# A scan and two expert layers on one core: one warm-up product, first weights loaded first and rounded early, fourth weight tile ahead of the sums' write, probabilities later

## The chip, the core and the metric

The kernel runs on one core of a Trainium2 chip. Its engines are TensorE (PE; its weight loads are shown as PEld), VectorE (DVE), ScalarE (ACT), GpSimd (POOL) and SyncE (SP), which here only issues transfers. The metric is the device time of one execution in microseconds. Each engine works through its own list of instructions in order; an instruction waits until what it needs has been signalled, and what stands behind it waits with it.

## What is computed

Three layers follow one another: a chunked scan with decay, a mixture of four experts with ReLU, and a dense layer with a gate. Cut to what matters:

```
log_a = log(clip(a, 1e-6, 1))                 # a: 4 x 8 heads x 768 positions
cum   = cumsum(log_a) within a chunk
M     = (C @ B^T) * exp(cum_i - cum_j), causal
y     = M @ x + (C @ state) * exp(cum)        # state carried over chunks
state = exp(sum log_a) * state + sum(B x^T * exp(cum_end - cum_j))
x     = y as 3072 tokens x 256
p     = domain_probs / sum(domain_probs)      # 3072 x 4
x     = sum_e p_e * (relu(x @ w1[e]) @ w2[e]) # F = 1024
out   = (silu(x @ wg) * (x @ wv)) @ wo        # F = 1536
```

The kernel uses chunks of 128 positions, which gives the same result.

## The kernel before

**Tiles.** The scan is done in 24 tiles of 128 tokens (`q` = 0 to 23). Each holds for 8 heads a table `L` of 128 x 128 decays, which is turned by ScalarE into exponentials and multiplied by scores (products of B and C). The products of these weights with x give the tokens of the expert layer. Experts 0 and 1 start as soon as the first two tiles of the scan are there; the other scan tiles are worked in between their products. A unit is one expert, one token block and one of eight columns of hidden features: six products of L616 into one of three banks `h`, from which ScalarE makes `hh` (ReLU, rounded, L657) and VectorE the rest `hl` (L658); three units later six products of L624 add up the output. A bank `h` is taken again three units later, when `hh` and `hl` are both made.

**Two parts of each number.** fp32 numbers are multiplied as a high part (rounded by ScalarE) and a low part (what is left, by VectorE or GpSimd). So each weight tile of 512 KB has to be loaded, rounded (`high`, L268, or L158) and subtracted (`low`, L272, or L162) before L616 or L624 can use it. A weight tile (e, part) is loaded by `expert_load` (L180); parts 0 and 2 are the first layer of expert e, parts 1 and 3 the second.

**The first two scan tiles** go a direct way in `begin` (from L284): warm-up products on `ones` (L1161), four masks (`first_mask`, L198), running sums of log a by a product with a triangle (`sums`, `cum`), rows of these sums added to the masks (`first_rows`, L205), scores (`first_scores`, L221), exponentials (`first_direct`, `first_exp`), weights (`first_weights`, L257), and then the products with x (`a_heads`, L539). The other tiles get their table `L` from DRAM: the sums are copied by ScalarE (`crow`, L328), written to `crow_d` (L329), and read back spread over all partitions (`a_load_cum`, L412). GpSimd cuts what lies above the diagonal (`a_causal`, L419), ScalarE takes exponentials (`a_exp`, L426). The scores of the third and fourth tile go into a bank `direct` (`direct_scores`, L221), which is the bank of the first two tiles' output and state sums `y01`; VectorE copies the state sums out as `st` (`a_keep`, L557).

**What sets the order.** The order on each engine is that of the code (`manual_schedule`); work between the units is put into numbered half-unit slots by `put`. All loads and writes named here go through SyncE's one list of transfers. [...] The probabilities are divided by their sum (`mixture`, L360 to L363), written to `probs_d` (L368) and read back spread (`pbc`, L652) in the middle of the first token block. `totals` computes on VectorE what ScalarE turns into `dec` (L282). `head_constants` computes three small tables (`csel`, `csgn`, `pairblk`) from `headsel`.

## Time and profile before

| | us |
|---|---|
| median of the timed runs (833.76, 833.8, 834.35) | 833.8 |
| the profiled execution | 834.19 |
| its span in the profile | 832.4 |
| TensorE busy | 822.5 (99%) |
| VectorE busy | 539.0 (65%) |
| ScalarE busy | 488.4 (59%) |
| GpSimd busy | 444.6 (53%) |

Busy time of TensorE includes instructions that overlap; a 99% share does not say that it runs at its peak. What counts is where TensorE has to wait, and on whom. The profile names a releaser for each wait; times are counted from the start of the span, and 1.8 us of the execution lie outside it.

### The profile page before, as it was taken

To read this page: it belongs to the slowest core of one execution; us is meant where nothing else is said; L and a number is where in the kernel's file an instruction comes from. 1 tells how busy PE (TensorE), PEld (TensorE's weight loads), DVE (VectorE), ACT (ScalarE), POOL (GpSimd) and SP (SyncE) were. 2 spreads that over 40 slices of the span, in tenths; PEclk is the share of its full clock that TensorE was granted. 3 is DMA by queue.
4 is the path that set the end of the run, shared out by engine and by line. 5 is a ranking of instruction groups with operands and counts; after the bars stand their busy time and mean duration, and the time that the engine had idled before them with its cause. 6 is when DMAs were issued, how large, how long until landed. Compare 5 with 4: busy or idle time off the path is not lost.

```text
span 832.4 us, 12687 instructions
## 1 busy us (share of the span) xinstructions
PE 822.5 (99%) x4417; PEld 683.7 (82%) x4417; DVE 539.0 (65%) x830; ACT 488.4 (59%) x977; POOL 444.6 (53%) x448
## 2 busy tenths in 40 slices
PE   8999999999999999999999999999999999999997
PEld 7998888888778888888888888888888888888886
DVE  6777668565245946665657576648667676676675
ACT  6888777666465566667766666654444444444343
POOL 2665775434397424687785355406756358444351
PEclk9999999999999999999999999999999999999999
DMA  7875546551210153544323231763544365427301
GB/s 245 273 238 160 165 153 196 190 173 50 89 39 30 41 196 120 171 143 132 118 96 121 95 120 48 251 262 133 179 158 159 123 224 184 157 96 257 109 1 52
DMA packets 53296, 119.61 MB, mean 144 GB/s; under 512 B 5424, under 2 KB 19824, under 8 KB 53232
## 3 DMA queue, kind: packets, MB, share of 16 engines
q1 hardware_dynamic: 53088, 118.67, 42.3%
q8 instruction: 35, 0.57, 0.3%
q14 instruction: 29, 0.24, 0.1%
q10 hardware_dynamic: 144, 0.13, 0.0%
HBM read 101.34 MB, written 17.45 MB: 143 GB/s over the span
## 4 chain that ended last, share of the span: by engine, by line
PE 95%; ACT 2%; DVE 1%; issue 1%; ACTq 0%; DVEq 0%
PE h L936 30%; PE h L616 10%; PE d L1042 10%; PE po L1042 10%; PE po L624 10%; PE d L936 8%; PE po L1125 6%; PE d L1125 6%; PE scores L468 1%; PE ypsum L539 1%; PE ypsum L484 1%; DVE acc L679 0%; ACT we_h L687 0%; PE ypsum L497 0%; PE direct L221 0%
## 5 line engine op out<-in xcount | busy, mean ns | idle before, releaser
L1097 POOL TENSOR_TENSOR al<-s,ah 128x512 fp32r<-128x512 f32 x70 | 102.6, 1489 | 144.1 <-ACT ah L1095 112.2
L1095 ACT ACTIVATE ah<-s 128x512 fp32r<-128x512 f32 x72 | 45.3, 632 | 83.4 <-DVE s L1090 83.4
L1007 DVE TENSOR_TENSOR d<-d,c 128x512 f32<-128x512 f32 x32 | 22.4, 699 | 101.5 <-ACT c L1004 101.5
L658 DVE SCALAR_TENSOR_TENSOR hl<-h,hh 128x512 fp32r<-128x512 f32 (+1 forms) x80 | 46.3, 583 | 59.7 <-ACT hh L657 59.4
L991 DVE SCALAR_TENSOR_TENSOR hl<-h,hh 128x512 fp32r<-128x512 f32 x96 | 66.1, 689 | 20.6 <-PE d L1042 15.8
L1042 PE MATMUL po<-hh,we_o 128*128 128x512 f32 x256 | 78.9, 389 | 0.5 <-DVE acc L679 0.5
L1042 PE MATMUL d<-hh,we_o 128*128 128x512 f32 x256 | 78.8, 389 | 0.0
L990 ACT ACTIVATE hh<-h 128x512 fp32r<-128x512 f32 x96 | 57.1, 597 | 27.7 <-DVE h L1011 23.3
L657 ACT ACTIVATE hh<-h 128x512 fp32r<-128x512 f32 (+1 forms) x80 | 40.2, 509 | 52.8 <-PE h L616 52.4
L1085 ACT ACTIVATE s<-s 128x512 f32<-128x512 f32 x54 | 34.0, 632 | 45.5 <-DVE s L1084 44.7
L426 ACT ACTIVATE L<-L,cum 128x128 f32<-128x128 f32 x176 | 56.0, 394 | 4.8 <-POOL L L419 4.8
L616 PE MATMUL h<-xh,w_h 128*128 128x512 f32 (+1 forms) x160 | 56.7, 354 | 1.3 <-DVE hl L658 0.8
L624 PE MATMUL po<-hh,w_h 128*128 128x512 f32 (+1 forms) x160 | 56.4, 353 | 0.6 <-DVE tmp L677 0.6
L1042 PEld LDWEIGHTS po<-hh,we_o 128*128 128x128 f32 x256 | 48.0, 188 | 10.8 <-ACT we_o L687 0.9
L1042 PEld LDWEIGHTS d<-hh,we_o 128*128 128x128 f32 x256 | 48.1, 188 | 10.0
L936 PE MATMUL h<-xh,wq_h 128*128 128x512 f32 x144 | 56.1, 390 | 0.0
L936 PE MATMUL h<-xh,wq_l 128*128 128x512 f32 x144 | 56.0, 389 | 0.0
L936 PE MATMUL h<-xl,wq_h 128*128 128x512 f32 x144 | 56.0, 389 | 0.0
L616 PE MATMUL h<-xl,w_h 128*128 128x512 f32 (+1 forms) x160 | 55.6, 348 | 0.0
L624 PE MATMUL po<-hl,w_h 128*128 128x512 f32 (+1 forms) x160 | 55.5, 347 | 0.0
L616 PE MATMUL h<-xh,w_l 128*128 128x512 f32 (+1 forms) x160 | 55.5, 347 | 0.0
L624 PE MATMUL po<-hh,w_l 128*128 128x512 f32 (+1 forms) x160 | 55.4, 346 | 0.0
(244 smaller groups left out, 2385.0 us busy)
## 6 DMA issues: line engine op xcount, KB each, us to landing
wq_h<-wd_d SPq DMA_DIRECT2D x36, 448.0 KB
wq_l<-wd_d SPq DMA_DIRECT2D x36, 448.0 KB
L<-crow_d SPq DMA_DIRECT2D x22, 512.0 KB
bc<-in_bc_dram SPq DMA_DIRECT2D x21, 512.0 KB
wq_o<-wo_d SPq DMA_DIRECT2D x18, 512.0 KB
raw_q<-in_w_dram SPq DMA_DIRECT2D x32, 256.0 KB
pbc<-probs_d SPq DMA_DIRECT2D x22, 256.0 KB
wd_d<-wd_h SPq DMA_DIRECT2D x12, 448.0 KB
```

The lines of the kernel that those rows point to most:

```text
L426: nc.scalar.activation(out=L[:, h, :], in_=L[:, h, :], func=AF.Exp, bias=cols(cum, q)[:, h:h + 1])
L616: nc.tensor.matmul(ps, w[:, k, fs], v[:, k, :], start=(i == 0), stop=(i == len(ops) - 1))
L624: nc.tensor.matmul(po[d], w[:, fc, dsl], x, start=(first and i == 0), stop=(last and i == 2))
L657: nc.scalar.activation(out=hh, in_=ph, func=AF.Relu)
L658: nc.vector.scalar_tensor_tensor(out=hl, in0=ph, scalar=0.0, in1=hh.bitcast(F32), op0=ALU.max, op1=ALU.subtract)
L936: nc.tensor.matmul(ps, x[:, ws], y, start=(start and i == 0), stop=(i == 2), skip_group_check=True)
L990: S.activation(out=hh, in_=ps, func=AF.Relu)
L991: return lambda: V.scalar_tensor_tensor(out=hl, in0=ps, scalar=0.0, in1=hh.bitcast(F32), op0=ALU.max, op1=ALU.subtract)
L1042: nc.tensor.matmul(po[d], both[:, z, dsl], y, start=(first and i == 0), stop=(last and i == 2), skip_group_check=True)
L1095: nc.scalar.activation(out=ah, in_=av, func=AF.Copy)
L1097: low.tensor_tensor(out=al, in0=av, in1=ah.bitcast(F32), op=ALU.subtract)
L1125: nc.tensor.matmul(po[d][:, z:z + n], x[:, dsl], y[:, z:z + n], start=(first and i == 0), stop=(last and i == 2), skip_group_check=True)
```

## The change

It has four parts.

1. One warm-up product on `ones` instead of three (each is two instructions in the profile).
2. The first weight tile (`raw`, expert 0, part 0) is loaded right after `a`, ahead of B and C of the first two tiles. Its high part is rounded in one instruction ahead of the exponentials, where before there were two halves in between and after them. Both low halves go to GpSimd, where the second was VectorE's. `pin` is loaded earlier.
3. The fourth weight tile (expert 0, part 3) is loaded with the first ones, ahead of the write of the sums, and the sums are copied and written before the last exponential of the first tiles.
4. `head_constants` moves from slot 3 into `begin`, its two selects on GpSimd into `constants`; `mixture` and its write move from slot 3 to slot 6, behind the loads of slot 5.

```
         keep(lower, ones, [[-1, P]], 0, 1, ALU.is_gt)
-
-
-    def head_constants():
         keep(headsel, headsel, [[-N, H]], 0, 1)
         keep(headsel, headsel, [[N, H]], N - 1, -1)
+
+
+    def head_constants():
...
         first_rows(rows)
+        head_constants()
         first_scores(0)
...
         mm(py[:, 320:], lower, la)
+        high, low = split_parts(0, 0)
+        high()
+        low(0, nc.gpsimd)
+        low(1, nc.gpsimd)
         first_direct(0, 0, rows[0])
...
         first_scores(1)
+        nc.scalar.activation(out=crow, in_=pr.rearrange("p (g i) -> p g i", g=2), func=AF.Copy)
+        nc.sync.dma_start(out=crow_d.rearrange("(g r) i -> r g i", g=2), in_=crow)
         for _ in range(2):
             mm(pt[:, 3 * P:], ones, ones)
-        high, low = split_parts(0, 0)
-        high(0)
         first_exp(1, 1)
-        high(1)
         first_weights(0, 1)
...
         first_weights(1, 0)
-        nc.scalar.activation(out=crow, in_=pr.rearrange("p (g i) -> p g i", g=2), func=AF.Copy)
-        nc.sync.dma_start(out=crow_d.rearrange("(g r) i -> r g i", g=2), in_=crow)
-        expert_load(0, 3, bacc[0])
         a_load(2)
...
-        low(0, nc.gpsimd)
         a_done_high(0)
-        low(1, nc.vector)
         a_done_low(0)
...
         nc.sync.dma_start(out=la, in_=a_d)
+        expert_load(0, 0)
         for q in range(NFIRST):
             a_load(q)
+            if q == 0:
+                nc.sync.dma_start(out=pin, in_=probs)
...
-        expert_load(0, 0)
...
         expert_load(0, 2, bacc[1])
-        nc.sync.dma_start(out=pin, in_=probs)
+        expert_load(0, 3, bacc[0])
...
-        for _ in range(3):
+        for _ in range(1):
             nc.tensor.matmul(first[0][0][:, :P], ones, ones, start=True, stop=True)
...
-        put(3, lambda: (head_constants(), mixture(), mixture_store()))
+        put(6, lambda: (mixture(), mixture_store()))
```

SyncE's transfers from the start, before (`acc_88` from `in_bc` is B and C of the first two tiles, `raw_0` the first weights, `acc_86` the fourth weight tile, `crow_d` the sums' write, the last `L` the third scan tile's table):

```order
L1147 DMA la<-in_a_dram 128x192
L390 DMA acc_88<-in_bc_dram 128x1024
L180 DMA raw_0_141<-in_w_dram 128x2x512
L403 DMA nat<-in_nat_dram 128x384 x2
L180 DMA raw_1_147<-in_w_dram 128x4x256
L180 DMA acc_87<-in_w_dram 128x2x512
L1156 DMA pin<-in_probs_dram 128x96
L329 DMA crow_d<-crow 96x2x128
L180 DMA acc_86<-in_w_dram 128x4x256
L390 DMA bc<-in_bc_dram 128x1024
L412 DMA L<-crow_d 128x1024
```

and now:

```order
L1146 DMA la<-in_a_dram 128x192
L180 DMA raw_0_136<-in_w_dram 128x2x512
L389 DMA acc_88<-in_bc_dram 128x1024
L1151 DMA pin<-in_probs_dram 128x96
L402 DMA nat<-in_nat_dram 128x384 x2
L180 DMA raw_1_148<-in_w_dram 128x4x256
L180 DMA acc_87<-in_w_dram 128x2x512
L180 DMA acc_86<-in_w_dram 128x4x256
L320 DMA crow_d<-crow 96x2x128
L389 DMA bc<-in_bc_dram 128x1024
L411 DMA L<-crow_d 128x1024
```

The first weights moved ahead of B and C, `pin` up behind them, the fourth weight tile from behind the sums' write to ahead of it.

ScalarE after its second table load, before (L253 and L248 are the exponentials of the first two tiles, `w_0_0_h` the rounded first weights):

```order
L291 ACTIVATE wj<-la 128x1
L253 ACTIVATE L<-po_164,cum 128x128 x4
L248 ACTIVATE L<-L 128x512 x2
L268 ACTIVATE w_0_0_h<-raw_0_141 128x512
L248 ACTIVATE L<-L 128x512
L268 ACTIVATE w_0_0_h<-raw_0_141 128x512
L328 ACTIVATE crow<-h_176 96x256
L578 ACTIVATE xh_78<-h_239 128x2x128
```

and now:

```order
L291 ACTIVATE wj<-la 128x1
L268 ACTIVATE w_0_0_h<-raw_0_136 128x1024
L253 ACTIVATE L<-po_165,cum 128x128 x4
L248 ACTIVATE L<-L 128x512 x2
L319 ACTIVATE crow<-h_177 96x256
L248 ACTIVATE L<-L 128x512
L577 ACTIVATE xh_78<-h_246 128x2x128
```

The rounding became one instruction ahead of all exponentials, and the copy `crow` moved ahead of the last of them.

VectorE in the first units, before (from the first `hl` shown to the copies `st`):

```order
L658 SCALAR_TENSOR_TENSOR hl<-h_304,hh 128x256
L141 TENSOR_REDUCE csel<-headsel 128x4
L144 TENSOR_TENSOR csgn<-csel 128x2
L146 TENSOR_TENSOR pairblk<-headsel 128x128
L360 TENSOR_REDUCE psm<-pin 128x24
L361 TENSOR_SCALAR psm<-psm 128x24
L362 RECIPROCAL psm<-psm 128x24
L363 TENSOR_TENSOR pn<-pin,psm 128x96
L658 SCALAR_TENSOR_TENSOR hl<-h_325,hh 128x256
L162 TENSOR_TENSOR w_0_1_l<-acc_86,w_0_1_h 128x1024
L658 SCALAR_TENSOR_TENSOR hl<-h_354,hh 128x256
L557 COPY st<-y_238 128x64 x2
```

and now:

```order
L657 SCALAR_TENSOR_TENSOR hl<-h_306,hh 128x256
L657 SCALAR_TENSOR_TENSOR hl<-h_317,hh 128x256
L162 TENSOR_TENSOR w_0_1_l<-acc_86,w_0_1_h 128x1024
L657 SCALAR_TENSOR_TENSOR hl<-h_346,hh 128x256
L359 TENSOR_REDUCE psm<-pin 128x24
L360 TENSOR_SCALAR psm<-psm 128x24
L361 RECIPROCAL psm<-psm 128x24
L362 TENSOR_TENSOR pn<-pin,psm 128x96
L556 COPY st<-y_245 128x64 x2
```

The three constants left this stretch, and the four instructions of the mixture (L360 to L363, now L359 to L362) moved behind two `hl` and a weight split, still ahead of `st`.

## Rows read from the trace of the kernel before

**Rows 1.** Waits of TensorE, whole run: us in total, times, longest.
```profile
PE direct L221 <- PE h L616: 0.8, 1, 0.8
PE h L616 <- DVE hl L658: 0.8, 1, 0.8
...
PE h L616 <- ACT xh L578: 0.5, 1, 0.5
```

**Rows 2.** TensorE's timeline: start, us, engine, line, out<-in, count, idle before and releaser.
```profile
1.12 1.65 PE L1161 MATMUL s<-ones 128*128 128x128 f32 x6 [1.12 <-DVE ones L126]
2.56 1.06 PE L198 MATMUL po<-above,upto 128*128 128x512 bf16 x2
...
4.26 0.63 PE L286 MATMUL h<-upper,spaced 128*128 128x128 f32 x2
...
5.37 0.58 PE L205 MATMUL po<-sums,pick 32*128 32x128 f32 x2 [0.23 <-DVE cum L297]
...
7.00 0.39 PE L205 MATMUL po<-sums,pick 32*128 32x128 f32 x2
...
7.21 1.07 PE L221 MATMUL s<-acc 16*128 16x128 f32 x16
...
12.97 0.39 PE L616 MATMUL h<-xh,w_h 128*128 128x256 f32 x1 [0.50 <-ACT xh L578]
```

**Rows 3.** Timeline of GpSimd and ScalarE, first 11 us.
```profile
1.39 0.29 POOL L123 TENSOR_SCALAR_AFFINE_SELECT above<-lower 128x128 bf16<-128x128 f32 x1
...
3.13 0.22 ACT L289 ACTIVATE spaced<-la 128x16 f32<-128x16 f32 x1 [1.05 <-DVE la L287]
...
7.40 1.15 ACT L253 ACTIVATE L<-po,cum 128x128 f32<-128x128 f32 x4 [2.15 <-PE h L205]
...
10.19 1.28 POOL L272 TENSOR_TENSOR w_l<-raw,w_h 128x512 fp32r<-128x512 f32 x1 [7.84 <-ACT w_h L268]
```

**Rows 4.** Stretches: engines' busy time, granted clock, DMA share, GB/s.
```profile
0.00:5.80 5.80, 4.45 (x22) 3.39 (x26) 1.14 (x7) 3.35 (x5) 1.41 (x9) 1.00 0.64 198
5.80:10.00 4.20, 4.20 (x66) 3.85 (x64) 2.55 (x5) 2.60 (x8) 0.00 (x0) 1.00 0.97 342
0.00:18.60 18.60, 16.74 (x178) 14.17 (x179) 11.64 (x31) 12.61 (x25) 3.79 (x14) 1.00 0.72 232
```

**Rows 5.** Timeline of SyncE's DMA queue and of GpSimd, 11 to 20 us.
```profile
11.69 0.34 SPq L329 DMA_DIRECT2D crow_d<-crow  x1
...
13.53 0.33 SPq L412 DMA_DIRECT2D L<-crow_d  x1
...
19.78 1.31 POOL L419 TENSOR_SCALAR_AFFINE_SELECT L<-L 128x1024 f32<-128x1024 f32 x1 [6.05 <-DMA L<-crow_d]
```

**Rows 6.** VectorE's timeline, 13 to 22 us.
```profile
13.90 0.69 DVE L272 TENSOR_TENSOR w_l<-raw,w_h 128x512 fp32r<-128x512 f32 x1 [0.28 <-ACT w_h L268]
...
17.05 0.15 DVE L141 TENSOR_REDUCE csel<-headsel 128x4 f32<-128x8 f32 x1
...
17.52 0.25 DVE L360 TENSOR_REDUCE psm<-pin 128x24 f32<-128x96 f32 x1
...
18.59 0.41 DVE L658 SCALAR_TENSOR_TENSOR hl<-h,hh 128x256 fp32r<-128x256 f32 x1
...
20.39 0.35 DVE L557 COPY st<-y 128x64 f32<-128x64 f32 x2
...
21.43 0.35 DVE L281 TENSOR_REDUCE dec<-totm 128x24 f32<-128x192 f32 x1
```

**Rows 7.** Timeline of ScalarE and VectorE, 21 to 27 us.
```profile
21.12 1.28 ACT L426 ACTIVATE L<-L,cum 128x128 f32<-128x128 f32 x4 [3.49 <-POOL L L419]
22.31 0.20 ACT L282 ACTIVATE dec<-dec 128x24 f32<-128x24 f32 x1
...
23.86 1.04 ACT L158 ACTIVATE w_h<-acc 128x1024 fp32r<-128x1024 f32 x1
...
26.07 0.42 DVE L658 SCALAR_TENSOR_TENSOR hl<-h,hh 128x256 fp32r<-128x256 f32 x1
```

## The prediction

> **What bounds the kernel now.** I read the waits of TensorE first, then its timeline up to its first steady work, then the other engines at each wait, then the DMA totals. TensorE is the bound: over the whole run it waits for others only in a handful of places, and the three that this change can reach are the 0.8 us before the product `direct`, the 0.8 us before an `h` of L616, and the 0.5 us before the first L616 [rows 1]. The others lie in later tiles, and I leave them as they are. A change at the start is therefore worth what it takes off the start of L616 at 12.97 plus what it takes off the two waits of 0.8.

> The start is a chain on TensorE [rows 2]: warm-up products at 1.12, four masks from 2.56, sums at 4.26, row products from 5.37, first scores at 7.21, L616 at 12.97. Two levels of the clock show in it. [...] The step lies at the end of the row products, about 7.1 us, after TensorE had been busy with one short wait since 1.12. The granted-clock column reads 1.00 from the first microsecond [rows 4], so only the durations show it.

> **Part 1, four of six warm-up instructions go.** They take 1.44 us before the first mask. With two left, TensorE is free at about 1.60, and the mask then waits for GpSimd's `above`, done at 1.39 + 0.29 = 1.68 [rows 3]. First mask at about 1.75, fourth done by 1.75 + 1.70 = 3.45. The sums need `spaced`, done at 3.13 + 0.22 = 3.35, and a weight load: 3.6 instead of 4.26. So 0.65 us comes off, and the row products move from 5.37 to 4.72. [...]

> **Part 2, the first weights load ahead of B and C.** The first scores need B and C (`acc` of L390). By 5.8 us the queue had moved 5.8 x 198 = 1.15 MB [rows 4]: `la` 0.10, B and C 0.52, `raw` 0.52. B and C were in the middle of that and nobody waited for them; now they are its end, 5.8 us and a lag. The lag from the last byte to the release is between nothing and that of a like transfer: 18.6 x 232 = 4.31 MB is what was issued up to `L` of the third tile, and its reader started at 19.78 [rows 4, 5], 1.15 us later. I take 1.0, the nearer row being another 512 KB in a full queue: landing at 6.8, first scores at 7.0. So of the 0.65 us only **0.2 us** is left. Without lag they start at 6.55, run at half clock to 7.1 and end about 0.4 us earlier than now. The other bound lies below nothing: in an execution where the clock rises well before 7.1, the old kernel would have run its row products faster and been at the scores by about 6.4 (eight rounds of 0.13 after 5.37), while the new one still stands at 7.0: 0.6 us lost. Range of this term: 0.6 lost to 0.4 gained.

> From the first scores to L616 the chain is TensorE's own order with short steps on VectorE and ScalarE and none of them is lengthened: the crow copy leaves ScalarE there, the low half leaves VectorE. So L616 starts at 12.97 - 0.2 = 12.77.

> **Part 3, rounding in ScalarE's gap.** ScalarE is idle for 2.15 us before 7.40 [rows 3]. The one rounding of 1,024 columns takes 1.04, as the like rounding at 23.86 does [rows 7]. Its data land at about 4.3 + 1.0, so it ends by about 6.4, ahead of the row products (about 6.7). Cost nothing; if the data came 0.5 us later it would push the first exponentials by 0.2, which have that much room. GpSimd's two low halves, 1.28 us each [rows 3], end by about 9.2, well before 12.8. The head constants go to VectorE's idle time at about 5: cost nothing there.

> **Part 4, the crow write earlier, the fourth weight tile ahead of it.** The sums' write is issued at 11.69, and the third tile's `L`, read back from it, at 13.53 [rows 5]. Now ScalarE copies crow after its third exponential, by my estimate at about 8.9, and the write is issued at about 9.3, but it queues behind all weights: 3.16 MB, at 342 GB/s from 5.8 on [rows 4] until 11.7. The write is over by 12.0, confirmed about 13.0, and `L` follows with only B and C of the third tile ahead of it in the queue, where before the fourth weight tile was ahead too. Taking 1.84 us from issue to use (the crow write's own, 11.69 to 13.53) and 1.5 us for 0.52 MB, it lands at about 16.5 to 17 instead of 19.78. GpSimd's mask (1.31) then ends about 18.2, and ScalarE's exponentials, which stood 3.49 us until 21.12 for it [rows 7], no longer wait.

> **Part 5, what is late next: VectorE.** Behind those exponentials ScalarE computes `dec`, which needs the end of VectorE's run from 13.90 to 21.78, in which VectorE hardly waits [rows 6]. Of this run the head constants go, 17.05 to 17.52, **0.47 us**. The mixture, 17.52 to 18.59, stays in the run, since it moves behind two `hl` and one weight split but remains ahead of the `st` copies at 20.39. Against L616 the copies come 0.47 us earlier; `direct` waits for them (its bank), so of that 0.8 us some 0.3 goes once the `hl` that stood behind the mixture (18.59) is also earlier. `dec` comes from 21.43 + 0.35 to 21.31 against the same L616 and ScalarE can run it at about 21.4, not at 22.31 [rows 7]: **0.9 us**. From there to the `hl` at 26.07 that frees the bank for the L616 which waited 0.8, ScalarE and VectorE work without a pause in the same order as before, so this `hl` comes 0.9 us earlier against the start. TensorE is ahead of it until then and still waits, about 0.4 instead of 0.8.

> The bank at 26.07 decides, not the sum of the two waits: 0.2 (start) + 0.9 (`dec`) = **1.1 us**. After it ScalarE and VectorE catch up with TensorE, and nothing in the waits speaks for giving it back.

> **Part 6, the probabilities later.** Their write now queues behind three more weight tiles, 1.57 MB or 4.6 us at 342 GB/s; the read-back that waits for it, and behind that on SyncE all loads of the fifth tile, I put at about 25.7 (an estimate: weights over near 24.2, then write, lag and issue). The queue runs empty for that while, so it loses its lead, and these loads arrive about when they did. I count nothing. The room is some 3 us before the first product with the probabilities; a loss would start there.

> **The sum.** 834.19 (profiled) - 1.1 = 833.1. The three timed runs have their median at 833.8, 0.4 below the profiled one; from it the sum gives 832.7. Since a kernel whose first scores wait for a transfer profits less from an early clock than the old one, I take the middle, **832.9 us**; the bounds of the start term alone (0.4 gained instead of 0.2, or 0.6 lost) give 832.7 to 833.7.

> **Rivals.** (a) *The clock rises later.* For it: less work before it, a pause between warm-up and masks, and a wait for B and C, all in the stretch before the step at 7.1. Against: the work removed is 1 us of the 6 before the step. [...]
> [...]

> (b) *`L` of the third tile comes no earlier,* because its source is written behind the weights. Then ScalarE waits as before, the bank is free at 26.49 whatever the start does, and the time is 833.8. It begins when `L` lands after 18.7 (21.3 less four exponentials and the mask); my 17 leaves 1.7 us. (c) *B and C land by 6.2 and the clock has risen:* the whole 0.65 stays, plus 0.9, plus a few tenths where TensorE no longer meets the waits: 832.0. (d) *The change does not do what it says:* `raw` lands too late for the gap and ScalarE delays the exponentials; 0.5 us dearer than forecast, 833.4, inside the forecast's range.

> **How the numbers follow.** Forecast 832.9 (832.2 to 833.7, d included) 0.64; (a) 834.9, 0.10; (b) 833.8, 0.11; (c) 832.0, 0.15. The range that leaves out a tenth at each end goes from 831.9 to 834.4. A difference of 0.2% (1.7 us, below 832.1 or above 835.5) is about what can be told from no change: faster 0.20 (most of c and a little of the forecast), slower 0.04 (the far end of a), same 0.76.

> **What would show it.** First mask near 1.75, sums near 3.6; first scores near 7.0 with a DMA as releaser; sixteen of them in about 1.1 us (clock up) or 2 us (rival a); first L616 near 12.8; GpSimd's mask of the third tile near 17 (rival b: near 20); `dec` near 21.2 with VectorE as releaser; the L616 that waited for the bank freed at 26.49 now near 25.4. I am wrong if that L616 has not moved, or if what it gains is given back before 60 us.

## The result, and the profile after

The changed kernel takes **838.15 us** (median; 837.56 to 839.14) beside 834.08 of the kernel before on the same chip: a ratio of 1.0052, 95% interval 1.0040 to 1.0064. It is slower by 4.1 us. The forecast was 832.9 with a range from 831.9 to 834.4, so it had the wrong sign, and the time lies 3.7 us above the range. The profiled execution of after took 837.56 us with a span of 835.8, 3.4 us above the span before; it is the fastest of the four, so the profile shows 3.4 us of the loss and not 4.1.

The waits of TensorE over the whole run (us in total, times, longest), beside [rows 1]:

```profile
PE direct L221 <- PE h L615: 0.8, 1, 0.8
...
PE h L615 <- DVE hl L657: 0.3, 1, 0.3
...
PE s L221 <- DMA acc<-in_bc_dram: 0.2, 1, 0.2
```

The wait for the bank fell from 0.8 to 0.3, the one before `direct` stayed, and a short one for B and C is new. By the waits alone the kernel should have gained some tenths. The loss is not a wait, and TensorE's timeline up to its steady work shows it (columns as in [rows 2]):

```profile
1.74 1.03 PE L198 MATMUL po<-above,upto 128*128 128x512 bf16 x2
...
3.52 0.77 PE L286 MATMUL h<-upper,spaced 128*128 128x128 f32 x2
...
4.76 0.58 PE L205 MATMUL po<-sums,pick 32*128 32x128 f32 x2 [0.23 <-DVE cum L297]
...
7.02 2.08 PE L221 MATMUL s<-acc 16*128 16x128 f32 x16 [0.17 <-DMA acc<-in_bc_dram]
...
11.35 2.08 PE L221 MATMUL po<-acc 16*128 16x128 f32 x16
...
16.95 0.38 PE L615 MATMUL h<-xh,w_h 128*128 128x256 f32 x1 [0.50 <-ACT xh L577]
...
17.63 0.28 PE L615 MATMUL h<-xh,w_h 128*128 128x256 f32 x1
17.75 0.28 PE L615 MATMUL h<-xh,w_l 128*128 128x256 f32 x1
```

Up to 7.02 all is as forecast: the first mask 0.82 us earlier than in [rows 2], the sums at 3.52 instead of 4.26, the row products at 4.76 instead of 5.37, the first scores at 7.02 with a DMA as releaser. But these sixteen products last 2.08 us where [rows 2] has 1.07, and the sixteen at 11.35 again 2.08. The clock is still at its lower level. The first L615 starts at 16.95 instead of 12.97, and only there do products of 256 columns follow each other at 0.12 us. The stretch from the first scores to the first L615 took 16.95 - 7.02 = 9.93 us instead of 12.97 - 7.21 = 5.76.

The granted clock does not show this in after, just as in [rows 4]: the clock records in these traces begin with the first rise (at 7.19 us in before, at 16.85 in after), and the column reads 1.00 where no record stands. TensorE is busy 5.98 of 6.00 us, and only the durations double:

```profile
1.12:7.00 5.88, 5.49 (x42) 3.69 (x42) 1.47 (x10) 4.25 (x7) 1.71 (x8) 1.00 0.75 256
7.00:13.00 6.00, 5.98 (x38) 5.32 (x40) 3.05 (x5) 2.96 (x8) 2.35 (x2) 1.00 0.96 326
```

What the rest of the change did can be read against the first L615. Here is after's timeline of ScalarE, SyncE's queue, GpSimd and VectorE, and of two products of TensorE that waited:

```profile
5.71 1.06 ACT L268 ACTIVATE w_h<-raw 128x1024 fp32r<-128x1024 f32 x1 [0.42 <-DMA raw<-in_w_dram]
6.84 1.15 ACT L253 ACTIVATE L<-po,cum 128x128 f32<-128x128 f32 x4
...
25.74 0.22 ACT L282 ACTIVATE dec<-dec 128x24 f32<-128x24 f32 x1 [3.25 <-DVE dec L281]
...
13.04 0.33 SPq L411 DMA_DIRECT2D L<-crow_d  x1
...
18.01 1.51 POOL L418 TENSOR_SCALAR_AFFINE_SELECT L<-L 128x1024 f32<-128x1024 f32 x1 [0.90 <-DMA L<-crow_d]
...
17.87 0.69 DVE L272 TENSOR_TENSOR w_l<-raw,w_h 128x512 fp32r<-128x512 f32 x1 [0.28 <-ACT w_h L268]
...
18.94 1.12 DVE L272 TENSOR_TENSOR w_l<-raw,w_h 128x512 fp32r<-128x512 f32 x1
...
25.35 0.35 DVE L281 TENSOR_REDUCE dec<-totm 128x24 f32<-128x192 f32 x1
...
29.99 0.39 PE L615 MATMUL h<-xh,w_h 128*128 128x256 f32 x1 [0.30 <-DVE hl L657]
...
50.68 0.36 PE L623 MATMUL po<-hh,w_h 128*128 128x256 f32 x1 [0.56 <-DVE tmp L676]
```

The same two products of TensorE before:

```profile
26.55 0.39 PE L616 MATMUL h<-xh,w_h 128*128 128x256 f32 x1 [0.78 <-DVE hl L658]
...
47.23 0.36 PE L624 MATMUL po<-hh,w_h 128*128 128x256 f32 x1 [0.56 <-DVE tmp L677]
```

The bank's L615 starts 29.99 - 16.95 = 13.04 us after the first one; before it was 26.55 - 12.97 = 13.58. So the change gained 0.54 us there. The sum: 3.98 lost at the start, 0.54 gained, 3.44 left. The next like wait of TensorE, 0.56 us for `tmp`, ends at 50.68 in after and at 47.23 in before, 3.45 apart, and the spans differ by 3.4. Nothing is won or lost behind it.

### The profile page after: what moved, and what is told of

It reads as the page before. It is cut to its first block, busy times and chain, and to the rows that moved or that the text cites. A ratio compares the mean times of both kernels' runs of the same rounds, so it can differ in the third digit from the quotient of the medians.

```text
span 835.8 us, 12679 instructions
## 1 busy us (share of the span) xinstructions
PE 826.2 (99%) x4413; PEld 686.3 (82%) x4413; DVE 538.9 (64%) x829; ACT 488.4 (58%) x976; POOL 446.4 (53%) x449
## 4 chain that ended last, share of the span: by engine, by line
PE 93%; ACT 2%; DVE 2%; issue 1%; DMA 1%; SPq 0%; ACTq 0%; DVEq 0%
PE h L935 30%; PE d L1041 10%; PE h L615 10%; PE po L1041 10%; PE po L623 9%; PE d L935 8%; PE po L1124 6%; PE d L1124 6%; PE scores L467 1%; PE ypsum L538 1%; PE ypsum L483 1%; DMA acc<-in_bc_dram 1%; DVE hl L657 0%; DVE acc L678 0%; ACT we_h L686 0%
## 5 line engine op out<-in xcount | busy, mean ns | idle before, releaser
L615 PE MATMUL h<-xh,w_h 128*128 128x512 f32 (+1 forms) x160 | 56.7, 354 | 0.8 <-ACT xh L577 0.5
L615 PE MATMUL h<-xl,w_h 128*128 128x512 f32 (+1 forms) x160 | 55.6, 347 | 0.0
L615 PE MATMUL h<-xh,w_l 128*128 128x512 f32 (+1 forms) x160 | 55.5, 347 | 0.0
```

The lines of the kernel that those rows point to most:

```text
L615: nc.tensor.matmul(ps, w[:, k, fs], v[:, k, :], start=(i == 0), stop=(i == len(ops) - 1))
```

## The experiments

Two groups of times run through all of this: executions in which the clock is up early and that take some 832 to 835 us, and executions in which it is late and that take 837 to 839. One kernel can have both. The kernel before was timed 73 times beside the experiments, 833.0 to 834.8, and was never late. One execution of each kernel has a trace; whether another was early or late is read from its time alone. The experiments ran on three chips, each with the kernel before timed beside them.

### One product, alone, and the change without it

The first pair does Part 1 alone and undoes Part 1 alone. Before with one product, the only edit:

```diff
-        for _ in range(3):
+        for _ in range(1):
             nc.tensor.matmul(first[0][0][:, :P], ones, ones, start=True, stop=True)
```

> The kernel before with one warm-up product instead of three, all else as before, so B and C come first and nobody waits for them. Theory A: the clock rises late all the same, the first scores take about 2.1 us, the first L616 starts near 16.5 and the time is 837.5. Theory B: no wait, the clock rises near 7.1, the start is earlier by up to 0.4 us, 833.4 to 834.0.

Measured: 837.77 us (837.47 to 839.28), ratio 1.0054, interval 1.0039 to 1.0069. TensorE's timeline of this kernel:

```profile
6.58 1.95 PE L221 MATMUL s<-acc 16*128 16x128 f32 x16
...
16.38 0.39 PE L616 MATMUL h<-xh,w_h 128*128 128x256 f32 x1 [0.50 <-ACT xh L578]
```

No transfer is waited for, B and C lie where they lay before, and the slow stretch is there all the same: 1.95 us for these scores and 2.08 for the next sixteen at 10.78, the first L616 at 16.38; the clock's record begins at 16.01. One edit of two warm-up calls gives the whole loss. (The profiled execution is the slowest of the four, 839.28: its clock also fell again, from 26.25 to 29.66.)

The changed kernel with three products again:

```diff
-        for _ in range(1):
+        for _ in range(3):
```

> The changed kernel with three warm-up products again (six instructions instead of two), all else as changed. Theory A, TensorE's clock rises late because work ahead of it is gone: the rise is back near 7.1 us, the sixteen first scores take about 1.1 us, the first L615 starts near 13.0 and the time is 833.5, since the 0.5 us won between the first L615 and the bank that frees near 26 stays. Theory B, the late rise comes from the wait for B and C: TensorE reaches the first scores at 7.2, after B and C have landed (6.8), so there is no wait and the same 833.5. Theory C, the early sums' write and the other moves cost time by themselves: 835 or more with the clock up.

Measured: 834.71 us, ratio 1.0018, interval 1.0007 to 1.0029. Eight of its ten runs lie between 833.46 and 835.13, two at 836.82 and 838.14. So the warm-up brings most of the loss back, but with B and C last in the queue (first scores at 7.48 after a wait of 0.37 for them) two runs in ten are still late.

### Where the wait for B and C comes in

After with B and C loaded ahead of the first weights again, one product kept; and the same with three products:

```diff
-        expert_load(0, 0)
         for q in range(NFIRST):
             a_load(q)
             if q == 0:
+                expert_load(0, 0)
                 nc.sync.dma_start(out=pin, in_=probs)
```

> The changed kernel with B and C loaded ahead of the first weights again, one warm-up product. The first scores have no wait; the rounding of the first weights then waits for them until about 6.8 and holds the first exponentials by about 1 us. Theory A: late rise, 838 to 839. Theory B: the clock is up near 7.1, and with the exponentials later the time is 833.5 to 834.5.

> The changed kernel with three warm-up products and B and C loaded first: both suspects undone. Theory A and B: clock up near 7.1, 833.3 to 834.3, the exponentials somewhat later than with the first weights first. Theory C: 835 or more.

Measured: with one product 837.17 us (ratio 1.0035, interval 1.0023 to 1.0046), two runs early (833.1 and 834.01) and eight late (836.96 to 837.35); with three products 833.84 us (ratio 1.0002, interval 0.9993 to 1.0012), all ten early. The profiled run of the first is one of the early two. Its last row products and first scores:

```profile
5.77 0.46 PE L205 MATMUL po<-sums,pick 32*128 32x128 f32 x2
...
6.20 0.34 PE L205 MATMUL po<-sums,pick 32*128 32x128 f32 x2
...
6.36 1.08 PE L221 MATMUL s<-acc 16*128 16x128 f32 x16
...
12.57 0.39 PE L615 MATMUL h<-xh,w_h 128*128 128x256 f32 x1 [0.50 <-ACT xh L577]
```

The scores last 1.08 us, and the row products shorten from 0.46 to 0.34 just ahead of them: the same kernel finds the clock up at 6.30 (by the clock's record) in one run and, by their times, not in eight others. With the clock up and one product the first L615 stands at 12.57, 0.4 us ahead of [rows 2]; how much of that is Part 1's and how much comes from a rise 0.9 us earlier than before, the run does not tell.

### How much warm-up, and when

Two products, five products, and one product with two more behind the row products:

```diff
-        for _ in range(1):
+        for _ in range(2):      # and 5 in the other kernel
```

```diff
         first_rows(rows)
+        for _ in range(2):
+            mm(pt[:, 3 * P:], ones, ones)
         head_constants()
```

> The changed kernel with two warm-up products. If the rise depends on how much TensorE worked in a stretch whose place differs from run to run, some executions are early (about 834) and some late (837 to 838), more of them late than with three products. If one product more is enough, all are near 834; if only the unbroken work up to the masks counts, all are late, since a short pause at the masks remains.

> The changed kernel with five warm-up products (ten instructions) instead of one, nothing else. Theory (the work of the first three microseconds decides when the clock rises, and the wait for B and C only adds to the risk): masks start 0.96 us later than with three (about 3.5), first scores near 8.0 without a wait for B and C, all runs in the early group, sixteen scores in 1.1 us, first L615 near 13.9, time 834.3, at most 835. Rival (the wait for B and C, or the order of the weights, is what delays the clock): there is no such wait here either, so this run alone does not exclude it, but some late runs (837 to 839) would remain if it is the order of the weights. Rival (only the total work up to 7 us counts): same early group; the filler run, with as much work later and 839.05, already speaks against it.

> The changed kernel with one warm-up product, and two products on ones put behind the row products, where TensorE stood for B and C: the same work as three warm-up products in all, but later, and no wait for B and C. If the total work up to about 7 us decides, or the wait, the clock is up early and the time near 834. If the work of the first three microseconds decides (the stretch that ends ahead of the row products), the rise stays late and the time is 838 or above.

Measured: two products 834.37 us (ratio 1.0021, interval 1.0005 to 1.0038), six early and four late; five products 833.91 us (ratio 1.0004, interval 0.9995 to 1.0013), all eleven early; one at the start and two later 839.05 us (ratio 1.0062, interval 1.0048 to 1.0076), all four late. With the runs above:

| products at the start | B and C | runs | late | rise in the profiled run, us |
|---|---|---|---|---|
| 3 (before) | ahead of the weights | 73 | 0 | 7.19 |
| 3 | ahead | 10 | 0 | 6.98 |
| 5 | behind | 11 | 0 | 4.34 |
| 3 | behind | 10 | 2 | 6.61 |
| 2 | behind | 10 | 4 | 4.29, fell at 7.70 |
| 1 | ahead | 10 | 8 | 6.30 |
| 1 (before with one) | ahead | 4 | 4 | 16.01 |
| 1 (after) | behind | 4 | 4 | 16.85 |
| 1, and 2 behind the row products | behind | 4 | 4 | 22.19 |

The last column is where the clock's record in the trace begins. The three kernels of the next section, also with three products and B and C ahead, add 33 runs, none late.

TensorE in the kernel with the two later products:

```profile
6.73 1.22 PE L286 MATMUL h<-ones 128*128 128x128 f32 x4
...
17.82 0.58 PE L617 MATMUL h<-xh,w_h 128*128 128x256 f32 x1 [0.50 <-ACT xh L579]
18.19 0.42 PE L617 MATMUL h<-xh,w_l 128*128 128x256 f32 x1
```

They fill the time in which the scores could not yet start, and the clock is not up even at the first L617 (0.58 where [rows 2] has 0.39, and 0.42 for the product behind it, which takes 0.28 at 17.75 in after). By the end of these two, at about 7.9 us, as many warm-up products had run as with three at the start. With all three at the start eight of ten runs were early, and with only two there, on the same chip as this kernel, six of ten. So the count of warm-up products run by 7.9 us does not decide; it matters that they run at the start.

The profiled run of the kernel with two products is a late one of another kind. Its timeline and its stretches (columns as in [rows 4]):

```profile
5.78 0.31 PE L205 MATMUL po<-sums,pick 32*128 32x128 f32 x2
...
7.17 1.63 PE L221 MATMUL s<-acc 16*128 16x128 f32 x16 [1.07 <-DMA acc<-in_bc_dram]
...
11.05 2.08 PE L221 MATMUL po<-acc 16*128 16x128 f32 x16
```

```profile
6.00:7.00 1.00, 0.09 (x4) 0.00 (x0) 0.88 (x2) 1.00 (x2) 0.00 (x0) 1.00 1.00 334
7.00:8.00 1.00, 0.83 (x12) 0.84 (x14) 0.41 (x1) 1.00 (x5) 0.98 (x1) 0.85 1.02 343
...
10.00:16.00 6.00, 6.00 (x56) 4.70 (x55) 2.31 (x5) 1.47 (x4) 0.00 (x0) 0.50 0.89 261
```

Here the clock was up before the row products: 0.31 us each, eight rounds of 0.11. Then TensorE did next to nothing (0.09 of a microsecond) from 6 to 7, waiting 1.07 us for B and C, and the granted clock fell in the middle of the scores, from 1.00 to 0.50 (at 7.70 by its record), and stayed there until 17.94. So the place of B and C may do harm in a way of its own: behind the wait that it makes, a clock that was already up came down. The rows are one run's, but every run has its mean granted clock on record, and it bears them out. A clock that is late from the start leaves the mean near 1.00 (after: 1.000 and 0.999), since no record stands there; this fall brought it to 0.992. Of the four late runs with two products three read 0.991 or 0.992, and the two late ones with three products and B and C behind read 0.995 and 0.991; the 73 runs of before never read less than 0.997. So five of these six late runs look like a fall and one like a late rise. The wait for B and C is not the only place for one: of the eight late runs with one product and B and C ahead, one reads 0.993. With three products, none of 116 runs was late with B and C ahead, and two of ten with them behind.

With five products the same wait was 0.56 us, and the clock stayed up:

```profile
4.26 0.64 PE L198 MATMUL h<-above,upto 128*128 128x512 bf16 x2
4.74 0.38 PE L286 MATMUL h<-upper,spaced 128*128 128x128 f32 x2
...
7.33 1.16 PE L221 MATMUL s<-acc 16*128 16x128 f32 x16 [0.56 <-DMA acc<-in_bc_dram]
...
13.19 0.39 PE L615 MATMUL h<-xh,w_h 128*128 128x256 f32 x1 [0.50 <-ACT xh L577]
```

The second pair of masks ends early (the sums follow after 0.48 us; in [rows 2] two masks take 0.85): the clock rose at about 4.4, by my estimate from these two numbers; its record begins at 4.34. The expectation had first scores at 8.0 without a wait. With the clock up this early the row products were done sooner, and the scores waited at 7.33.

### What the rest of the change is worth, and a faster version

The whole change but Parts 1 and 2 of the prediction, with the rounding in halves behind the exponentials again (three products and B and C first, as in the edits above; cut to the rounding):

```diff
-        high, low = split_parts(0, 0)
-        high()
-        low(0, nc.gpsimd)
-        low(1, nc.gpsimd)
...
+        high, low = split_parts(0, 0)
+        high(0)
         first_exp(1, 1)
+        high(1)
+        low(0, nc.gpsimd)
+        low(1, nc.gpsimd)
```

> The changed kernel with three warm-up products, B and C first, and the first weights rounded in halves behind the exponentials again (both low halves on GpSimd): what is left of the change is the early sums' write, the fourth weight tile ahead of it, the head constants and the later probabilities. The clock is up early, the first L615 starts near 13.0, and the bank that freed at 26.49 frees about 0.5 us earlier: 833.1 against 833.6 of before. If these moves are worth nothing, 833.6.

Measured: 833.66 us, ratio 0.9997, interval 0.9988 to 1.0006: no difference. In its profiled run the first L616 stands at 12.23, 0.74 us ahead of [rows 2], and that is given back. The lead comes with the clock, which rose at 5.64 here and at 7.19 in before, with the same warm-up ahead of it. TensorE, VectorE and GpSimd there, and the stretches behind:

```profile
5.68 0.29 PE L205 MATMUL po<-sums,pick 32*128 32x128 f32 x2
...
18.93 0.99 DVE L363 TENSOR_TENSOR pn<-pin,psm 128x96 f32<-128x96 f32 x1
...
18.72 1.09 POOL L419 TENSOR_SCALAR_AFFINE_SELECT L<-L 128x1024 f32<-128x1024 f32 x1 [5.78 <-DMA L<-crow_d]
...
20.29 1.16 PE L221 MATMUL direct<-bc 16*128 16x128 f32 x16 [1.28 <-issue]
...
23.06 0.41 PE L624 MATMUL po<-hh,w_h 128*128 128x256 f32 x1
23.27 0.41 PE L624 MATMUL po<-hh,w_l 128*128 128x256 f32 x1
```

```profile
22.00:23.00 1.00, 1.00 (x9) 1.00 (x9) 0.22 (x1) 1.00 (x5) 0.86 (x1) 0.85 1.12 373
23.00:24.00 1.00, 1.00 (x7) 1.00 (x6) 0.10 (x1) 1.00 (x2) 0.23 (x1) 0.50 1.06 373
...
26.00:27.00 1.00, 1.00 (x10) 1.00 (x9) 1.00 (x3) 1.00 (x2) 0.00 (x0) 0.94 0.34 58
```

The mixture's last step (L363) starts 0.21 us after GpSimd's mask and takes 0.99 us, where the same step takes 0.32 at 24.07 in after. So `st`, which follows it on VectorE, is late, and TensorE stands 1.28 us ahead of `direct`. The profile names no releaser there; `direct` starts 0.1 us after `st` ends, as it does before (20.39 + 0.35 and 20.84). Then come the sixteen narrow products, and at 22.7 the granted clock falls to 0.50 until 26.1. Products that started every 0.12 us start every 0.21. This fall alone does not explain the median: four of the eleven runs have a mean granted clock of 1.000 and take 833.15 to 834.03 all the same.

So the mixture was moved out of this run of VectorE, into its idle time while TensorE does the row products (5.74 to 6.89 us), with the probabilities loaded second (edits beside the kernel above):

```diff
         head_constants()
+        mixture()
+        mixture_store()
         first_scores(0)
...
         nc.sync.dma_start(out=la, in_=a_d)
+        nc.sync.dma_start(out=pin, in_=probs)
...
-                nc.sync.dma_start(out=pin, in_=probs)
...
-        put(6, lambda: (mixture(), mixture_store()))
```

> As the kernel with halves behind the exponentials, but the probabilities are loaded second and divided on VectorE in its idle time ahead of the row products, and written then. If VectorE's run of instructions up to dec is what TensorE waits for, 1.07 us more leave that run: dec waits for the exponentials of the third tile instead, the wait before direct goes, the bank frees 1.5 us earlier than before, 832.0. If the third tile's table is the bound, nothing more than with the halves: 833.1. If the load of the probabilities ahead of B and C costs, the first scores start later than 7.2.

Measured: 832.76 us, ratio 0.9988, interval 0.9979 to 0.9996; all eleven runs early. It beats before by 1.0 us, and after by some 5; 832.0 was expected. `direct` no longer waits, but the bank's product does. VectorE, GpSimd and TensorE:

```profile
17.01 1.22 DVE L162 TENSOR_TENSOR w_l<-acc,w_h 128x1024 fp32r<-128x1024 f32 x1
...
23.02 2.11 DVE L162 TENSOR_TENSOR w_l<-acc,w_h 128x1024 fp32r<-128x1024 f32 x1 [1.70 <-ACT w_h L158]
...
17.11 2.07 POOL L421 TENSOR_SCALAR_AFFINE_SELECT L<-L 128x1024 f32<-128x1024 f32 x1 [3.81 <-DMA L<-crow_d]
...
22.97 1.09 POOL L421 TENSOR_SCALAR_AFFINE_SELECT L<-L 128x1024 f32<-128x1024 f32 x1 [1.62 <-DMA L<-crow_d]
...
25.53 0.38 PE L618 MATMUL h<-xh,w_h 128*128 128x256 f32 x1 [1.28 <-DVE hl L660]
```

Both directions of the collision stand here. At 17.01 VectorE was first, kept its 1.22 us, and the mask took 2.07 instead of 1.09. At 22.97 the mask was first, kept its 1.09, and the low half of expert 1's weight took 2.11 instead of 1.22. The `hl` behind it came late, and TensorE waited 1.28 us. The last run puts this weight behind the `hl`:

```diff
-        for part, slot, engines in ((0, 8, (nc.vector,)), ...
+        for part, slot, engines in ((0, 10, (nc.vector,)), ...
```

> The version with the mixture ahead of the row products, but expert 1's first weight tile is split (ScalarE's rounding, VectorE's low half) behind the next hidden column instead of ahead of it. In the run before it the low half L162 at 23.02 took 2.11 us instead of 1.23 beside GpSimd's mask 22.97 to 24.06, and the L618 at 25.53 waited 1.28 us for the `hl` behind it. Theory (the collision and the place of the low half set this wait, and nothing behind it needs the split so early): the L618 starts near 24.3 without a wait, and the run takes 832.8 - 1.2 = 831.6 us, slower by at most 0.3 where the next `hl`, now behind the low half, is late. Rival (what is gained there is given back at the next `hl`, which then stands behind rounding and low half): a wait of about 1 us at the following L618, and 832.8. Second rival (the next limit is the arrival of weights): 832.4.

Measured: 832.65 us, ratio 0.9986, interval 0.9977 to 0.9995: not told apart from the run before, and not the 831.6 that the theory gave. VectorE and TensorE:

```profile
24.31 1.22 DVE L162 TENSOR_TENSOR w_l<-acc,w_h 128x1024 fp32r<-128x1024 f32 x1
...
25.58 0.39 PE L618 MATMUL h<-xh,w_l 128*128 128x256 f32 x1 [0.63 <-DVE w_l L162]
```

The low half now takes 1.22 us, so this collision is gone, but the products at 25.58 use this very weight and wait 0.63 us for it. The theory had overlooked that the weight is due there. A wait of 1.28 became one of 0.63, and this profiled run began 0.35 us later (12.95 instead of 12.60, its clock having risen at 7.14 instead of 6.41), which hides the rest in it. It also has a collision of its own: the mask was first at 17.03, and the low half that the run before did in 1.22 us at 17.01 took 1.84 at 17.36. Why the medians differ by no more than 0.1 is not settled.

## Why the prediction was wrong

**Part 1, four warm-up instructions go.** The times up to the row products were right to 0.1 us, and the 6.55 at which the scores could start without a wait is 6.58 in before with one product. The failed step is the one that followed: the prediction kept the rise of the clock at 7.1 us and moved the work against it, and so put the first L616 at 12.77. In after the clock rose at 16.85 and the first L615 stands at 16.95. The rise hangs on this very work: before with one product, which changes nothing else, is slower by 0.54%. What about the two calls the clock reacts to stays open. Without them there is less work, and TensorE also stands still for about 0.1 us ahead of the first mask and ahead of the sums (an estimate from the spacing of the instructions); no run takes the one without the other.

**Rival (a), the clock rises later.** This is what came. It was seen, with what speaks for it, and given 0.10. "The work removed is 1 us of the 6 before the step" was the argument that failed: the share of the work says little: the table goes from no late run in 83 (three products, B and C ahead) to 20 in 22 (one product at the start). Its price failed too. In 834.9 stand 2.2 us for the lower clock (833.8 - 1.1 + 2.2), an estimate of the author's that no run shows. In its place the runs show 4.17 us: the stretch from the first scores to the first L615 holds 5.76 us of work at full speed and took 9.93, so a microsecond of it lost 0.42. A loss that ends at 12.97, where the stretch ended before, counts too little, since the stretch grows while it is slow. With the start as measured and the forecast's 0.9 at the bank the sum is 834.19 + 3.98 - 0.9 = 837.3, beside 837.56 profiled.

The moment of the rise is no fixed one: it stands at 5.64 to 7.19 us in the six profiled runs with three products, and with one product and B and C ahead two of ten runs were early. The 3.4 us that the profiled run lost are 0.4% of the span, but three times the whole sum of this change, 1.1 us: a share that is small beside a kernel can be large beside an edit.

**Part 2, the first weights ahead of B and C.** The landing was right: 6.8 forecast, scores at 7.02 measured. (The lag of the like transfer, put at 1.15 us, is about 1.2 by its own numbers, 19.78 - 18.6; nothing hangs on it.) That nothing but this moment was at stake was too little: behind the wait the clock came down again in the profiled run with two products, and by their mean clocks in four more late runs with two or three. What the part costs alone is the step from the kernel with three products and B and C first (all early, 833.84) to that with three and B and C last (two late in ten, 834.71); the two intervals still overlap, and in the first of them the rounding comes late (Part 3). The forecast's other bound, an early clock of which the old kernel has more, is what the kernel with five products shows: its scores wait for B and C until 7.33 with the clock long up. For the terms of this range, half the clock and 0.13 us a round, the runs show 1.95 us for the scores at 6.58 in before with one product, beside 1.07 in [rows 2], and rounds of 0.11 in the kernel with two products.

**Part 3, rounding in the gap.** Right: rounding from 5.71 to 6.77, the exponentials at 6.84 without a wait. With B and C first it would not have been free: in that kernel with three products the rounding waited until 7.31 for `raw`.

**Part 4, the sums' write.** The mechanism was right, the size not. `L` is issued at 13.04 instead of 13.53, though the start lost nearly 4 us, and the mask starts at 18.01 instead of 19.78. Forecast were 16.5 to 17, from an issue at about 13.0, which came true: from issue to use it took 4.97 us, not the 1.84 + 1.5 that were added up. Rival (b) did not come: ScalarE's `dec` waits for VectorE, as forecast.

**Part 5, VectorE's run.** 0.9 forecast, 0.54 measured, and the rest has a name. From the first L615 to `dec` VectorE needed 25.35 - 16.95 = 8.40 us, before 21.43 - 12.97 = 8.46. The constants are gone (0.47), but the low half at 18.94 takes 1.12 us where the one at 17.87 takes 0.69, since GpSimd's mask runs from 18.01 to 19.52: 0.43 back. The mask that comes earlier by Part 4 falls on work that it used to miss. The five-product kernel agrees in time with its own collision: there L360, behind a mask from 18.27 to 19.77, takes 0.46 instead of 0.18 and ends at 19.80, and the run to `dec` 21.45 - 13.19 = 8.26, which is 8.46 - 0.47 + 0.28.

Not everything on VectorE beside a mask was slowed: in the five-product kernel L359 at 19.06 took 0.24 us, in after, with no mask beside it, 0.23; and the `hl` at 18.60 in after took its 0.42. Of those that were slowed, L162, L272 and L363 have two tensors as input, and L360, with 0.46 instead of 0.18, has one. What makes a pair collide no run shows.

**Part 6, the probabilities later.** No loss was seen: the waits behind 30 us are the same. No run tests it apart.

**The sum.** With the clock up early, the two kernels nearest to the change gain nothing that can be measured: 833.91 with five products and 833.84 with three and B and C first, ratios 1.0004 and 1.0002. Against the profiled run of before, the five-product kernel is ahead by 0.44 us at the `tmp` wait (46.79 instead of 47.23), but that run of before was itself 0.6 above the median of its kind (834.19 beside 833.6). How the early runs of the two kernels differ below 0.1% stays open.

**Rivals (c) and (d)** did not come: B and C did not land by 6.2 us, and the first exponentials were not held up.

## What to carry to other kernels

Work whose result nobody needs may still be paid for: before taking warm-up away, ask what comes up late if the clock does, and price the whole stretch at the lower level, with its end moving along. Tell clock levels by the durations of like products (2.08 and 1.07 us for the sixteen scores here), and time such a change in many runs, since its effect may come in some of them only. Where an edit makes one engine's work earlier, look at what it will newly run beside: here VectorE's L162 took 2.11 us instead of 1.22 beside GpSimd's mask, and the mask 2.07 instead of 1.09 beside L162.
